# x's high halves made on ScalarE from raw x, and W's first chunk loaded by parts, in an FNet + GEGLU kernel

## The chip, the cores and the metric

One core of a Trainium2 chip runs the kernel. The metric is the device time of one execution in microseconds; the time before is the median of three runs. Names as in the profile: PE is TensorE's matmul, PEld its weight load, DVE VectorE, ACT ScalarE, POOL GpSimd, SP SyncE, whose queue issues the DMAs.

## The reference

```
h  = x + Real(DFT_seq(DFT_hidden(layernorm(x))))     x: 2048 x 448
     y = dft_seq_re @ a - dft_seq_im @ b,  a = ln @ dft_hid_re.T,  b = ln @ dft_hid_im.T
h2 = h + (gelu(ln(h) @ w_gate) * (ln(h) @ w_up)) @ w_down      w_gate, w_up: 448 x 1792
```

All in float32. The case here is the first product: the 2048 x 2048 sequence matrices (re and im), called W below, with the normalized x.

## The kernel before, in words

Float32 operands are split into two float16 halves, a high one (a rounded copy, made on ACT by `hi_part`, L103) and a low one (the difference, made on DVE by `lo_part`, L107 and L109). A product takes three matmuls: high by high, x's low by W's high, x's high by W's low (`TERMS`, L400).

The sequence transform runs in four batches of 512 output columns, each over 16 chunks of 128 rows of x (`N_STEPS` = 64 steps of the loop at L551). For each chunk the 448 columns of x are three blocks of 128 and a leftover of 64. `seq_mm` (L403) does the three blocks for both parts (re and im) in 18 matmuls of 128x512; `seq_mm_rest` (L418) does the leftover, in pairs that share PE. In the first batch x is loaded, normalized and split chunk by chunk, and kept in float16 for the other three batches; W is streamed in all four, two chunks of a batch sharing two 512 KB blocks (`seq_w`, L395: a chunk reads a part of both blocks). So chunk 6 needs the halves of blocks 6 and 7.

The order on every engine is written out by hand (`manual_schedule`). Ahead of the loop (L527 to L550) the first loads are issued (x tile 0, then the pieces of W's first two blocks and x tiles 1 and 2, then W's blocks 2 to 4) and the work of chunks 0 and 1 is interleaved. In the loop's step n, SP gets `x_load(n+3)` and `seq_load(n+5)`, and then, for the tiles ahead, come `x_norm(n+2)`, `seq_hi(n+3)`, `x_stats(n+3)`, `x_lo(n+2)`, `seq_lo(n+3)`. Steps 7, 9 and 11 also split the hidden transform's weights (`wh_split`, L455).

- `x_stats` (L340): mean and variance on DVE (L117, L118), the root on ACT (L124).
- `x_norm` (L344): on DVE the reciprocal and four small operations that refine it (`rstd`, L131 to L135) and the normalized x in place (`normed`, L140); on ACT x's high half from it.
- `x_lo` (L351): x's low half on DVE. x's raw tiles rotate through three buffers; the buffer of tile i is free after it.
- `first_load`, `first_hi`, `first_lo` (L374 to L393): blocks 0 and 1 of W in four pieces of 256 KB, by chunk and block, and their halves. These take two of the five buffers of W's raw blocks.

Chunks 0 to 2 are multiplied term by term over both parts (all high products first); from chunk 3 on part by part, with all three terms of a column block together, so the third matmul of such a chunk already reads W's low half. The leftover columns follow after chunks 1, 3, 7, 11 and 15.

Of the kernel before, what the change touches and what calls it, by code (L numbers as in the profile page):

```python
# [8 lines left out]
F16 = mybir.dt.float16  # L9
F32 = mybir.dt.float32  # L10
AF = mybir.ActivationFunctionType
ALU = mybir.AluOpType

P = 128
S, D, DF = 2048, 448, 1792
NT = S // P
# [6 lines left out]
EPS = 1e-5  # L23


X_SC = 16.0
D_SC = 64.0
# [5 lines left out]
def kernel(  # L33
# [35 lines left out]
    nc = tc.nc  # L69
    V, A, G, PE = nc.vector, nc.scalar, nc.gpsimd, nc.tensor  # L70
# [3 lines left out]
    small = ctx.enter_context(tc.tile_pool(name="small", bufs=3))  # L74
# [27 lines left out]
    def hi_part(dst, src, scale=1.0):  # L102
        A.activation(dst, src, AF.Copy, scale=scale)  # L103

    def lo_part(dst, src, hi, scale=1.0):
        if isinstance(scale, float) and scale == 1.0:
            V.tensor_sub(dst, src, hi)  # L107
        else:
            V.scalar_tensor_tensor(dst, src, scale, hi, op0=ALU.mult, op1=ALU.subtract)  # L109

    def stats(src, tag, pool=small):

        n = src.shape[1]
        mv = pool.tile([P, n, 2], F32, tag=f"mv{n}" if pool is small else f"mv_{tag}", name=f"mv_{tag}")
        for g in range(n):
            st = small.tile([P, 6], F32, tag="st", name=f"st_{tag}_{g}")
            V.bn_stats(st, src[:, g, :])  # L117
            V.bn_aggr(mv[:, g, :], st)  # L118
        return mv

    def root(mv, tag):
        n = mv.shape[1]
        sd = small.tile([P, n], F32, tag=f"sd{n}", name=f"sd_{tag}")
        A.activation(sd, mv[:, :, 1], AF.Sqrt, scale=1.0 / X_SC**2, bias=eps_t)  # L124
        return sd

    def rstd(mv, sd, tag, pool=small):

        n = sd.shape[1]
        r = pool.tile([P, 4, n], F32, tag=f"r{n}" if pool is small else f"r_{tag}", name=f"r_{tag}")  # L130
        V.reciprocal(r[:, 0], sd)  # L131
        V.tensor_scalar(r[:, 1], mv[:, :, 1], EPS, -0.5 / X_SC**2, op0=ALU.add, op1=ALU.mult)
        V.tensor_mul(r[:, 2], r[:, 0], r[:, 0])
        V.tensor_mul(r[:, 2], r[:, 2], r[:, 1])
        V.scalar_tensor_tensor(r[:, 3], r[:, 2], 1.5, r[:, 0], op0=ALU.add, op1=ALU.mult)  # L135
        return r[:, 3]

    def normed(dst, src, mv, r, g):

        V.tensor_scalar(dst, src, mv[:, g, 0:1], r[:, g : g + 1], op0=ALU.subtract, op1=ALU.mult)  # L140
# [147 lines left out]
    dft = right.enter_context(tc.tile_pool(name="dft", bufs=1, side="right"))  # L288
# [45 lines left out]
    xt, xs, norm_x = {}, {}, {}  # L334

    def x_load(i):
        xt[i] = dft.tile([P, 1, D], F32, tag="xt", bufs=3, name=f"x{i}")
        nc.sync.dma_start(xt[i][:, 0, :], x[i * P : (i + 1) * P, :])

    def x_stats(i):  # L340
        mv = stats(xt[i], f"x{i}")
        norm_x[i] = mv, root(mv, f"x{i}")

    def x_norm(i):  # L344
        mv, sd = norm_x.pop(i)
        xn = xt[i][:, 0, :]
        normed(xn, xn, mv, rstd(mv, sd, f"x{i}"), 0)
        xs[i] = dft.tile([P, 2, D], F16, name=f"xs{i}")
        hi_part(xs[i][:, 0], xn)

    def x_lo(i):  # L351
        lo_part(xs[i][:, 1], xt[i][:, 0, :], xs[i][:, 0])

# [1 line left out]
    wr, ws = {}, {}  # L357

    def seq_load(n):
        wr[n] = dft.tile([P, 8 * P], F32, tag="wr", bufs=5, name=f"wr{n}")  # L360
        b, q, jj = n // NT, n // 2 % 8, n % 2
        nc.sync.dma_start(wr[n], w_seq[(2 * b + jj) * 8 + q])

    def seq_hi(n):
        if n % 2 == 0:
            ws[n // 2] = dft.tile([P, 2, 2, 8 * P], F16, tag="ws", bufs=4, name=f"ws{n // 2}")
        hi_part(ws[n // 2][:, 0, n % 2], wr[n], D_SC)

    def seq_lo(n):
        t = ws[n // 2][:, :, n % 2]  # L370
        lo_part(t[:, 1], wr[n], t[:, 0], D_SC)


    def first_load(c, jj):  # L374
        if c == 0:
            wr[jj] = dft.tile([P, 8 * P], F32, tag="wr", bufs=5, name=f"wr{jj}")
        if c == jj == 0:
            ws[0] = dft.tile([P, 2, 2, 8 * P], F16, tag="ws", bufs=4, name="ws0")
        cols = slice(c * P, (c + 1) * P)
        nc.sync.dma_start(wr[jj].rearrange("p (b t) -> p b t", b=4)[:, :, cols], w_seq[jj * 8][:, :, cols])  # L380

    def first_views(c, jj):
        cols = slice(c * P, (c + 1) * P)
        ts = [wr[jj], ws[0][:, 0, jj], ws[0][:, 1, jj]]
        return [t.rearrange("p (b t) -> p b t", b=4)[:, :, cols] for t in ts]

    def first_hi(c, jj):
        src, hi, lo = first_views(c, jj)
        hi_part(hi, src, D_SC)

    def first_lo(c, jj):
        src, hi, lo = first_views(c, jj)
        lo_part(lo, src, hi, D_SC)  # L393

    def seq_w(n, l, part):  # L395

        t = ws[n // 2][:, l].rearrange("p a (r g c t) -> p r c a g t", r=2, g=2, c=2)
        return t[:, part, n % 2]

# [3 lines left out]
    def seq_mm(n, parts, terms=range(3)):  # L403

        b, c = divmod(n, NT)
        for part in parts:
            for k in range(3):
                for m in terms:
                    lx, lw = TERMS[m]
                    PE.matmul(  # L410
                        acc[b, 3 * part + k],
                        xs[c][:, lx, k * P : (k + 1) * P],
                        seq_w(n, lw, part),
                        start=c == 0 and m == 0,
                        stop=c == NT - 1 and m == 2,
                    )

    def seq_mm_rest(ns):  # L418

        for n in ns:  # L420
            b, c = divmod(n, NT)
            for m, (lx, lw) in enumerate(TERMS):
                for part in range(2):
                    PE.matmul(  # L424
                        acc[b, 6][64 * part : 64 * part + 64, :],
                        xs[c][:, lx, 3 * P :],
                        seq_w(n, lw, part),
                        start=c == 0 and m == 0,
                        stop=c == NT - 1 and m == 2,
                        skip_group_check=True,  # L430
                    )

    z = {}
# [67 lines left out]
    for k, f in enumerate(reversed(range(NF))):  # L501
        n = 17 + 3 * k
# [4 lines left out]
    for b in range(NB):  # L507
        for j in range(2):
            n = (b + 1) * NT + 1 + 6 * j
# [16 lines left out]

    x_load(0)  # L527
    for c in range(2):
        for jj in range(2):
            first_load(c, jj)  # L530
        x_load(c + 1)
    for n in range(2, 5):
        seq_load(n)
    x_stats(0)
    first_hi(0, 0)
    first_hi(0, 1)
    x_norm(0)
    first_lo(0, 0)
    x_lo(0)
    x_stats(1)  # L540
    first_lo(0, 1)
    first_hi(1, 0)
    first_hi(1, 1)
    x_norm(1)
    first_lo(1, 0)
    x_lo(1)
    first_lo(1, 1)
    seq_hi(2)
    x_stats(2)
    seq_hi(3)  # L550
    for n in range(N_STEPS):  # L551
        b, c = divmod(n, NT)
        if c == 0:
            for k in range(7):
                acc[b, k] = ps_seq.tile([P, TB], F32, tag="mm", name=f"acc{b}_{k}")
        if n + 3 < NT:
            x_load(n + 3)
        if n + 5 < N_STEPS:
            seq_load(n + 5)

        if n + 2 < NT:
            x_norm(n + 2)
        if 0 < n < N_STEPS - 3:
            seq_hi(n + 3)
        if n + 3 < NT:
            x_stats(n + 3)
        if n + 2 < NT:
            x_lo(n + 2)
        if n == 0:
            seq_lo(2)  # L570
        if n + 3 < N_STEPS:
            seq_lo(n + 3)
        for what in early.get(n, ()):
            what()
        if n < 3:
            for m in range(3):
                seq_mm(n, range(2), (m,))
        for part in range(2):
            if n >= 3:
                seq_mm(n, (part,))  # L580
            if c == NT - 1:
                for k in range(3 * part, 3 * part + 3):
                    z_out(b, k)
            for what in after.get((n, part), ()):
                what()

        if n in (1, 3) or n > 3 and c % 4 == 3:
            seq_mm_rest(range(n - 1 if n < 4 else n - 3, n + 1))
        if c == NT - 1:
            z_out(b, 6)  # L590
    gw = {f: gu[f].w for f in range(3)}
# [342 lines left out]
    for t in range(3 * NF, N_GU):  # L934
        f = t % NF
        if f < NF - 1:
            n, k = divmod(f, 2)
# [28 lines left out]
    for t in range(N_GU):  # L966
        q, f = divmod(t, NF)
# [58 lines left out]
    for i in range(4):  # L1026
        j, g = divmod(i, 2)
# [68 lines left out]
```

## Time and profile before

| | |
|---|---|
| median of three runs | 728.22 us (728.07 to 730.27) |
| the profiled execution | 729.39 us |
| its span | 727.6 us |
| first batch (16 chunks) | until about 81 us |
| ACT busy | 271.5 us (37%) |
| DVE busy | 500.1 us (69%) |
| TensorE's granted clock | 1.0 |

How to read it: a row of the timeline is the start in us from the start of the span, the duration, the engine, the line of the kernel, the operation, out<-in, shapes and the number of instructions merged; in brackets the idle time of the engine before it and what ended it. A row of the groups is line, engine, operation, out<-in, shapes and number, then busy us, mean ns of one, idle us before and what ended most of it. The chain of waits is followed back from the last instruction: start, duration, what. SPq is the queue that issues DMAs.

### The profile page before, as it was taken

Reading aid. Unit: us, or ns where it says so; the run is one execution under the profiler, and the core shown is the slowest. Engines: PE = TensorE matmul, PEld = TensorE weight load, DVE = VectorE, ACT = ScalarE, POOL = GpSimd, SP = SyncE. Lnnn points to the kernel's source line nnn. Section 1 sums busy time; section 2 is a strip of 40 time slices with the busy share of each in tenths; the row PEclk is TensorE's granted clock in tenths of the full one; section 3 lists DMA queues with packets and bytes.
Section 4 is the critical chain, followed back from the end, with each engine's and each line's share of the span. In section 5 each row is a group of like instructions: output and inputs, shape, how many; then the busy total and the mean of one; then the engine's idle time right before and its main releaser. Section 6 shows DMA issues by size and latency. Waiting matters only on the chain.

```text
span 727.6 us, 13421 instructions
## 1 busy us (share of the span) xinstructions
PE 719.5 (99%) x5330; PEld 499.2 (69%) x5330; DVE 500.1 (69%) x1026; ACT 271.5 (37%) x535; POOL 234.3 (32%) x274
## 2 busy tenths in 40 slices
PE   8999999999999999999999999999999999999998
PEld 5444444444444444444488889999999999999998
DVE  6888657486665866440477778788787877989730
ACT  4444704156133452221144443443444433454410
POOL 0000000000000001000057865577676766858430
PEclk9999999999999999999999999999999999999999
DMA  8766566577657976621057754757538496556411
GB/s 278 227 223 223 176 224 202 183 215 271 232 195 225 305 249 246 245 91 37 26 173 271 245 180 173 196 179 209 187 113 262 163 210 221 193 205 203 153 39 39
DMA packets 63518, 139.83 MB, mean 192 GB/s; under 512 B 30304, under 2 KB 39520, under 8 KB 63456
## 3 DMA queue, kind: packets, MB, share of 16 engines
q1 hardware_dynamic: 63456, 138.99, 58.0%
q8 instruction: 41, 0.67, 0.4%
q14 instruction: 21, 0.17, 0.1%
HBM read 112.23 MB, written 20.19 MB: 182 GB/s over the span
## 4 chain that ended last, share of the span: by engine, by line
PE 94%; DMA 3%; DVE 1%; ACT 1%; issue 0%; SPq 0%; DVEq 0%
PE acc L410 33%; PE pY L714 13%; PE acc_d L658 11%; PE y L475 9%; PE pX L714 9%; PE pZ L714 9%; PE acc L424 6%; DMA gw<-w_dram 2%; PE last_Y L877 1%; PE last_X L877 1%; PE last_tr L877 1%; DMA x<-in_x_dram 1%; PE last_a L877 1%; PE last_Z L877 1%; DMA wr<-in_w_seq_dram 1%; DVE ws L109 0%
## 5 line engine op out<-in xcount | busy, mean ns | idle before, releaser
L410 PE MATMUL acc<-ws,xs 128*128 128x512 f16 x1152 | 254.1, 379 | 0.9 <-ACT xs L103 0.6
L714 PEld LDWEIGHTS <-gw 128*128 128x128 f16 x2067 | 201.6, 98 | 24.9 <-DMA gw<-w_dram 2.1
L410 PEld LDWEIGHTS <-xs 128*128 128x128 f16 x1152 | 111.2, 98 | 139.6 <-issue 6.1
L714 PE MATMUL pY<-hops,gw 128*128 128x256 f16 x901 | 123.0, 273 | 1.6 <-DVE u L724 1.5
L658 PE MATMUL acc_d<-wd,dn_w 128*128 128x224 f16 x882 | 105.1, 259 | 0.0
L201 POOL TENSOR_TENSOR wd_s<-wd 128x448 f32<-128x448 f32 x7 | 7.9, 1131 | 274.1 <-DVE gu_w L109 274.1
L109 DVE SCALAR_TENSOR_TENSOR ws<-wr,ws 128x1024 f16<-128x1024 f32 (+1 forms) x66 | 77.9, 1187 | 15.2 <-ACT ws L103 15.2
L103 ACT ACTIVATE ws<-wr 128x1024 f16<-128x1024 f32 (+1 forms) x66 | 66.2, 1019 | 57.4 <-DMA wr<-in_w_seq_dram 28.0
L658 PEld LDWEIGHTS <-dn_w 128*128 128x128 f16 x882 | 85.1, 98 | 2.8
L714 PE MATMUL pX<-hops,gw 128*128 128x256 f16 x583 | 81.0, 273 | 1.0 <-DMA gw<-w_dram 0.9
L714 PE MATMUL pZ<-hops,gw 128*128 128x256 f16 x583 | 79.2, 273 | 0.0
L781 POOL TENSOR_TENSOR hh<-hh,g 128x256 f32<-128x256 f32 x42 | 31.0, 738 | 144.5 <-DVE hh L724 143.4
L724 DVE SCALAR_TENSOR_TENSOR u<-pY,u 128x256 f32<-128x256 f32 x112 | 46.9, 419 | 27.9 <-ACT c L788 19.0
L475 PE MATMUL y<-wh,z 128*128 128x448 f16 x336 | 65.7, 352 | 0.0
L483 DVE SCALAR_TENSOR_TENSOR hx<-y,hx 128x448 f32<-128x448 f32 x16 | 10.0, 625 | 78.1 <-PE y L475 78.1
L752 ACT ACTIVATE u<-pX 128x256 f32<-128x256 f32 x56 | 21.4, 383 | 90.9 <-PE pX L714 90.7
L475 PEld LDWEIGHTS <-z 128*128 128x128 f16 x336 | 32.8, 98 | 31.6 <-issue 0.4
L107 DVE TENSOR_TENSOR dn_w<-dn_s,dn_w 128x640 f16<-128x640 f32 x42 | 53.0, 1261 | 1.6 <-ACT dn_w L103 1.2
L765 ACT ACTIVATE g<-pX 128x256 f32<-128x256 f32 x56 | 21.4, 383 | 74.4 <-PE pX L714 69.1
L790 POOL TENSOR_TENSOR hh<-hh,c 128x256 f32<-128x256 f32 x42 | 40.8, 972 | 17.3 <-ACT c L788 17.1
L424 PE MATMUL acc<-ws,xs 128*64 128x512 f16 x384 | 44.7, 381 | 0.0
L807 POOL TENSOR_TENSOR dn_s<-hh 128x256 f32<-128x256 f32 x42 | 43.6, 1038 | 0.0
(107 smaller groups left out, 806.0 us busy)
## 6 DMA issues: line engine op xcount, KB each, us to landing
gw<-w_dram SPq DMA_DIRECT2D x53, 896.0 KB, 4.8
wr<-in_w_seq_dram SPq DMA_DIRECT2D x62, 512.0 KB, 5.9
w_dram<-gu_w SPq DMA_DIRECT2D x14, 896.0 KB, 4.7
gu_raw<-in_w_gu_dram SPq DMA_DIRECT2D x28, 384.0 KB, 5.8
wd<-in_w_down_dram SPq DMA_DIRECT2D x14, 448.0 KB, 5.4
x<-in_x_dram SPq DMA_DIRECT2D x16, 224.0 KB, 3.1
hx<-in_x_dram SPq DMA_DIRECT2D x8, 448.0 KB, 6.7
h_dram<-hx SPq DMA_DIRECT2D x8, 448.0 KB, 3.0
```

The costliest lines, as they stand in the source:

```text
L103: A.activation(dst, src, AF.Copy, scale=scale)
L107: V.tensor_sub(dst, src, hi)
L109: V.scalar_tensor_tensor(dst, src, scale, hi, op0=ALU.mult, op1=ALU.subtract)
L410: PE.matmul(acc[b, 3 * part + k], xs[c][:, lx, k * P : (k + 1) * P], seq_w(n, lw, part), start=c == 0 and m == 0, stop=c == NT - 1 and m == 2,
L424: PE.matmul(acc[b, 6][64 * part : 64 * part + 64, :], xs[c][:, lx, 3 * P :], seq_w(n, lw, part), start=c == 0 and m == 0, stop=c == NT - 1 ...
L475: PE.matmul(y[:, :D], z[b][:, lz, k, i * P : (i + 1) * P], wh[:, lw, k, :], start=k == 0 and m == 0, stop=k == 6 and m == 2,)
L658: PE.matmul(acc[k // 2][:, k % 2 * HD : (k % 2 + 1) * HD], a_of(la, a), b_of(lb, b), start=first and m == 0 and k % 2 == 0, stop=last and ...
L714: PE.matmul(ps, w[:, wl, wa + ws, :], ops[:, m + ms, :], start=first and n == 0, stop=last and n == len(terms) - 1, skip_group_check=True,)
L724: V.scalar_tensor_tensor(dst, ps, SC, other, op0=ALU.mult, op1=ALU.add)
L790: G.tensor_mul(c22, c22, self.c12)
L807: G.tensor_add(s[:, 0:2], t[:, 0:2], t[:, 2:4])
L877: PE.matmul(banks[0][:, c * HD : (c + 1) * HD] if one else banks[c][:, 0:HD], last["h"][:, lh, f, tok], w, start=f == 0 and m == 0 and c = ...
```

## The change

Three things change, all in the first batch.

W's blocks 0 and 1 are loaded in eight pieces of 128 KB, by chunk and part (re or im), into a tile of their own that takes the place of the later `z` tile; the five buffers of raw W blocks are left to blocks 2 and up. A part's halves are laid out next to each other.

x's high half is made by ACT straight from the raw tile, as Identity with a scale (1/deviation) and a bias (-mean/deviation) per partition, `x_hi`. The normalized x, which the low half is taken from, is made by a second such ACT operation in place, `x_norm`; for tile 0 it is made on DVE into a tile of its own. The small operations on DVE are four after the root in place of five, and one before it.

Chunks 0 to 5, and not 0 to 2, take all high products first; the leftover columns follow after chunks 0, 3, 7, 11 and 15.

```diff
     def x_stats(i):
         mv = stats(xt[i], f"x{i}")
-        norm_x[i] = mv, root(mv, f"x{i}")
+        sd = root(mv, f"x{i}")
+        r = small.tile([P, 5], F32, tag="rx", name=f"r_x{i}")
+        V.tensor_scalar(r[:, 1:2], mv[:, :, 1], EPS, -0.5 / X_SC**2, op0=ALU.add, op1=ALU.mult)
+        norm_x[i] = mv, sd, r
+    def x_rstd(i):
+        mv, sd, r = norm_x[i]
+        V.reciprocal(r[:, 0:1], sd)
+        V.scalar_tensor_tensor(r[:, 2:3], r[:, 0:1], r[:, 0:1], r[:, 1:2], op0=ALU.mult, op1=ALU.mult)
+        V.scalar_tensor_tensor(r[:, 3:4], r[:, 2:3], 1.5, r[:, 0:1], op0=ALU.add, op1=ALU.mult)
+        V.scalar_tensor_tensor(r[:, 4:5], mv[:, :, 0], -1.0, r[:, 3:4], op0=ALU.mult, op1=ALU.mult)
+    def x_hi(i):
+        r = norm_x[i][2]
+        xs[i] = dft.tile([P, 2, D], F16, name=f"xs{i}")
+        A.activation(xs[i][:, 0], xt[i][:, 0, :], AF.Identity, scale=r[:, 3:4], bias=r[:, 4:5])
     def x_norm(i):
-        mv, sd = norm_x.pop(i)
-        xn = xt[i][:, 0, :]
-        normed(xn, xn, mv, rstd(mv, sd, f"x{i}"), 0)
-        xs[i] = dft.tile([P, 2, D], F16, name=f"xs{i}")
-        hi_part(xs[i][:, 0], xn)
+        mv, sd, r = norm_x.pop(i)
+        x, xt[i] = xt[i][:, 0, :], xt[i][:, 0, :]
+        if i == 0:
+            xt[i] = dft.tile([P, 12 * P], F32, tag="raw", bufs=2, name="xn0")[:, :D]
+            normed(xt[i], x, mv, r[:, 3:4], 0)
+        else:
+            A.activation(xt[i], x, AF.Identity, scale=r[:, 3:4], bias=r[:, 4:5])
...
+    def first_load(c, part):
+        if c == part == 0:
+            wr["first"] = dft.tile([P, 2, 2, 4 * P], F32, tag="z", name="wr_first")
+            ws[0] = dft.tile([P, 2, 2, 8 * P], F16, tag="ws", bufs=4, name="ws0")
+        dst = wr["first"][:, part, c].rearrange("p (a g t) -> p a g t", a=2, g=2)
+        for jj in range(2):
+            nc.sync.dma_start(dst[:, jj], w_seq[8 * jj][:, 2 * part : 2 * part + 2, c * P : (c + 1) * P])
...
     x_load(0)
     for c in range(2):
-        for jj in range(2):
-            first_load(c, jj)
+        for part in range(2):
+            first_load(c, part)
         x_load(c + 1)
     for n in range(2, 5):
         seq_load(n)
     x_stats(0)
     first_hi(0, 0)
+    x_rstd(0)
+    x_hi(0)
+    x_norm(0)
     first_hi(0, 1)
-    x_norm(0)
-    first_lo(0, 0)
     x_lo(0)
     x_stats(1)
+    first_lo(0, 0)
+    first_hi(1, 0)
     first_lo(0, 1)
-    first_hi(1, 0)
+    x_rstd(1)
+    x_hi(1)
+    x_norm(1)
     first_hi(1, 1)
-    x_norm(1)
+    x_stats(2)
+    x_lo(1)
+    x_rstd(2)
+    x_hi(2)
+    x_norm(2)
     first_lo(1, 0)
-    x_lo(1)
     first_lo(1, 1)
     seq_hi(2)
-    x_stats(2)
     seq_hi(3)
...
-        if n + 2 < NT:
+        if 2 < n + 2 < NT:
+            x_rstd(n + 2)
+            x_hi(n + 2)
             x_norm(n + 2)
         if 0 < n < N_STEPS - 3:
             seq_hi(n + 3)
...
-        if n < 3:
+        if n < 6:
             for m in range(3):
                 seq_mm(n, range(2), (m,))
         for part in range(2):
-            if n >= 3:
+            if n >= 6:
                 seq_mm(n, (part,))
...
-        if n in (1, 3) or n > 3 and c % 4 == 3:
-            seq_mm_rest(range(n - 1 if n < 4 else n - 3, n + 1))
+        if n == 0 or c % 4 == 3:
+            seq_mm_rest(range(max(n - 3, min(n, 1)), n + 1))
```

More of the change, by code (lines that the diff above doesn't have):

```diff
@@ L341, in x_stats @@
         mv = stats(xt[i], f"x{i}")
-        norm_x[i] = mv, root(mv, f"x{i}")
-    def x_norm(i):
-        mv, sd = norm_x.pop(i)
-        xn = xt[i][:, 0, :]
-        normed(xn, xn, mv, rstd(mv, sd, f"x{i}"), 0)
-        xs[i] = dft.tile([P, 2, D], F16, name=f"xs{i}")
-        hi_part(xs[i][:, 0], xn)
+        sd = root(mv, f"x{i}")
[12 more added lines that the diff above has]
+        A.activation(xs[i][:, 0], xt[i][:, 0, :], AF.Identity, scale=r[:, 3:4], bias=r[:, 4:5])
+    def x_norm(i):
+        mv, sd, r = norm_x.pop(i)
[5 more added lines that the diff above has]
+            A.activation(xt[i], x, AF.Identity, scale=r[:, 3:4], bias=r[:, 4:5])
     def x_lo(i):
-        lo_part(xs[i][:, 1], xt[i][:, 0, :], xs[i][:, 0])
+        lo_part(xs[i][:, 1], xt[i], xs[i][:, 0])
     wr, ws = {}, {}
@@ L371, in seq_lo, with first_view, first_hi, first_lo @@
         lo_part(t[:, 1], wr[n], t[:, 0], D_SC)
[L374 to L377, printed above, removed]
+    def first_load(c, part):
+        if c == part == 0:
+            wr["first"] = dft.tile([P, 2, 2, 4 * P], F32, tag="z", name="wr_first")
             ws[0] = dft.tile([P, 2, 2, 8 * P], F16, tag="ws", bufs=4, name="ws0")
[L379 to L393, printed above, removed]
+        dst = wr["first"][:, part, c].rearrange("p (a g t) -> p a g t", a=2, g=2)
+        for jj in range(2):
+            nc.sync.dma_start(dst[:, jj], w_seq[8 * jj][:, 2 * part : 2 * part + 2, c * P : (c + 1) * P])
+    def first_view(l, c, part):
+        return ws[0].rearrange("p l a t -> p l (a t)")[:, l, (2 * part + c) * 4 * P :][:, : 4 * P]
+    def first_hi(c, part):
+        hi_part(first_view(0, c, part), wr["first"][:, part, c], D_SC)
+    def first_lo(c, part):
+        lo_part(first_view(1, c, part), wr["first"][:, part, c], first_view(0, c, part), D_SC)
     def seq_w(n, l, part):
+        if n < 2:
+            return first_view(l, n, part)
         t = ws[n // 2][:, l].rearrange("p a (r g c t) -> p r c a g t", r=2, g=2, c=2)
```

## The prediction

> **What bounds the kernel now.** I read the page first.
>
> ```profile
> span 727.6 us, 13421 instructions
> PE 719.5 (99%) x5330; PEld 499.2 (69%) x5330; DVE 500.1 (69%) x1026; ACT 271.5 (37%) x535; POOL 234.3 (32%) x274
> ```
>
> PE is busy for 719.5 of 727.6 us: 8.1 us of idle time is all that a better start can win, and a delay of PE is paid one for one. The change touches only the first of four batches (16 chunks, up to about 81 us), so I went to the chain of work that ended last.
>
> ```profile
> 7.54 7.23 DMA x<-in_x_dram
> ...
> 14.79 0.64 DVE st_x L117
> ...
> 20.94 3.84 PE acc L410 x17
> ...
> 34.54 7.50 PE acc L410 x34
> ```
>
> Two things are to be seen. Before 21 us the chain isn't PE's: it is the landing of x's fourth tile at 14.77, then DVE's queue in order (its statistics at 14.79, then the low part of tile 2, two low parts of W, and the reciprocal for tile 3 at 18.33, a row shown below). After that it is PE, but with one touch at 34.54: PE stood for the low part of W's chunk 7. So DVE is hardly ahead of PE. Why shows in the timeline of one step (chunk) of the loop:
>
> ```profile
> 18.33 0.15 DVE L131 RECIPROCAL r_x<-sd_x 128x1 f32<-128x1 f32 x1
> ...
> 22.35 0.16 DVE L131 RECIPROCAL r_x<-sd_x 128x1 f32<-128x1 f32 x1
> ...
> 22.93 0.16 DVE L135 SCALAR_TENSOR_TENSOR r_x<-r_x 128x1 f32<-128x1 f32 x1
> 23.12 0.51 DVE L140 TENSOR_SCALAR x<-x,mv_x,r_x 128x448 f32<-128x448 f32 x1
> 23.67 0.58 ACT L103 ACTIVATE xs<-x 128x448 f16<-128x448 f32 x1 [2.31 <-DVE x L140]
> 24.15 1.04 ACT L103 ACTIVATE ws<-wr 128x1024 f16<-128x1024 f32 x1
> 25.22 1.22 DVE L109 SCALAR_TENSOR_TENSOR ws<-wr,ws 128x1024 f16<-128x1024 f32 x1 [0.32 <-ACT ws L103]
> 26.36 0.15 DVE L131 RECIPROCAL r_x<-sd_x 128x1 f32<-128x1 f32 x1
> ```
>
> This is a ring between DVE and ACT: reciprocal, normalize, then on ACT x's high half (+1.32 after the reciprocal) and W's high half (+1.80), then on DVE W's low half (+2.87), and the next reciprocal behind it (+4.01). ACT waits 2.31 us of each step, but in this place it is part of the ring: what it gets longer there, the step gets longer.
>
> PE's own pace, from its timeline:
>
> ```profile
> 44.68 15.71 PE L410 MATMUL acc<-ws,xs 128*128 128x512 f16 x72
> 63.04 15.71 PE L410 MATMUL acc<-ws,xs 128*128 128x512 f16 x72
> ```
>
> Four chunks take 63.04 - 44.68 = 18.36 us, 4.59 per chunk, with 0.216 between two matmuls. A plain ring step is 4.0, but three steps also split the hidden weights:
>
> ```profile
> 42.44 0.16 DVE L131 RECIPROCAL r_x<-sd_x 128x1 f32<-128x1 f32 x1
> ...
> 48.19 0.16 DVE L131 RECIPROCAL r_x<-sd_x 128x1 f32<-128x1 f32 x1
> ...
> 66.59 0.16 DVE L131 RECIPROCAL r_x<-sd_x 128x1 f32<-128x1 f32 x1
> ```
>
> Step 7 takes 48.19 - 42.44 = 5.75, and step 9, with the same operations, is put at as much. From step 1 (18.33) to step 12 (66.59) are 48.26 us; less eight plain steps of 4.02 and these two, 4.6 are left for step 11 with the small last part. The ring's mean is 4.39, under PE's 4.59. An increase of 0.2 us per step makes the ring the bound of the batch.
>
> **The change, part by part.** The price of what moves to ACT stands in the groups by form, and one pair of such instructions in ACT's timeline:
>
> ```profile
> L103 ACT ACTIVATE xs<-x 128x448 f16<-128x448 f32 x16 | 9.2, 576 | 32.9 <-DVE x L140 32.8
> L222 ACT ACTIVATE xn_h<-hx,nb_h,r_h 128x448 f32<-128x448 f32 x8 | 5.7, 753 | 2.3 <-DVE nb_h L220 2.2
> L103 ACT ACTIVATE wh<-wh_raw,sign_t 128x448 f16<-128x448 f32 x1 | 0.7, 654 | 0.0
> 434.40 1.41 ACT L222 ACTIVATE xn_h<-hx,nb_h,r_h 128x448 f32<-128x448 f32 x2 [1.32 <-DVE nb_h L220]
> ```
>
> The same 128x448 costs 576 ns with constants, 654 with a scale per partition, 753 with scale and bias per partition. The new x_hi and x_norm are of the last kind (Identity, scale r[3], bias r[4]); x_hi writes f16, so its bounds are 0.58 and 0.75. I take 0.75, its nearest row by operands. Of two in a row the second starts 1.41 - 0.75 = 0.66 later. On the Trainium skill: its page "ScalarE: Activation LUTs", section "Step-by-step: what each stage is for", calls the scale and bias a free affine; taken at its word the two would cost the 576 of a copy. The rows speak against it, and so does the same page's section "What ACT_TABLE_LOAD costs", which adds about 93 ns for each per-partition operand; (753 - 576)/2 = 88 here.
>
> *The ring step after.* DVE: reciprocal, then three dependent small operations at the spacing of L135 and L140 above (0.19 each: 0.19, 0.39, 0.58), the last ends at +0.74. x_hi on ACT at +0.78, with the 0.04 from the end of L140 (23.63) to 23.67, until +1.53. x_norm overwrites the tile that x_hi reads, and in the changed program's order it waits for ACT itself: +1.56, not overlapped. W's high half 0.66 later, +2.22; W's low half 1.07 behind (24.15 to 25.22), +3.29, done at +4.52; the next reciprocal 1.14 behind its start, +4.43. So 4.42 for 4.01: the normalize that DVE saves (0.51) and a small product are more than eaten by 0.75 + 0.66 on ACT in place of 0.48. The low part of x (needs x_norm, +2.3) fits in front of W's low half. With the wh steps 0.41 longer each: 6.15, 6.15, 5.0.
>
> *The start.*
>
> ```profile
> 1.20 1.34 SPq L380 DMA_DIRECT2D wr<-in_w_seq_dram  x2
> 4.57 0.16 DVE L131 RECIPROCAL r_x<-sd_x 128x1 f32<-128x1 f32 x1 [0.36 <-ACT sd_x L124]
> 4.91 0.63 ACT L103 ACTIVATE ws<-wr 128x512 f16<-128x512 f32 x1 [0.38 <-DMA wr<-in_w_seq_dram]
> 5.17 1.48 SPq L362 DMA_DIRECT2D wr<-in_w_seq_dram  x3
> 5.76 0.63 ACT L103 ACTIVATE ws<-wr 128x512 f16<-128x512 f32 x1 [0.21 <-DMA wr<-in_w_seq_dram]
> 6.91 7.94 PE L410 MATMUL acc<-ws,xs 128*128 128x512 f16 x36 [0.61 <-ACT xs L103]
> 16.20 4.47 PE L410 MATMUL acc<-ws,xs 128*128 128x512 f16 x19
> 20.93 3.35 PEld L410 LDWEIGHTS <-xs 128*128 128x128 f16 x17 [0.56 <-DVE xs L107]
> GB/s 0 47 222 234 321 259 231 272 313 358 311 422 407 399 404 409 204 207 170 270 127 16 255 347 135 28 245 325 160 17 269 349 370 355 309 308 189 40 231 361
> DMA to landing us min/median/max: 3.7/5.4/8.1
> ```
>
> Now the first matmul needs both 256 KB pieces (the second's high half begins at 5.76). Afterwards it needs half of them, as many bytes as the first piece: high half at 4.91 to 5.54, x_hi at 5.45 (rstd done at 5.31) to 6.2, PE at 6.26, 0.65 earlier. The other part's high half is made until about 6.75 or 6.95, and PE wants it at 6.91. That gain doesn't last. ACT's queue now runs x_hi(1), x_norm(1), W(1,1), root(2), x_hi(2), x_norm(2) and only then the high halves of chunks 2 and 3, each 1.04: by the prices above they end near 16.3 (an estimate), and chunk 2's first matmul reads both, so PE starts chunk 2 about there, for 16.20 before. And the chain from x's fourth tile is untouched: SP issues it behind the same bytes. SP has four more pieces to issue at 0.67 (1.34 for two), so the three 512 KB loads begin at 5.17 + 2.7 = 7.9, the first lands no earlier than 3.7 (the shortest of such a load) later (11.6), and 1.25 MB more at 400 GB/s give 14.7 for x's fourth tile: 14.77 stands. Behind it one more small operation (0.13 to 0.2, the former L132 now sits before tile 2's low part): reciprocal of step 1 at 18.53 for 18.33. The term-major order for chunks 3 to 5 takes away PE's wait for tile 3's low part (0.56 at 20.93), yet chunk 3 can start only with x_hi(3) at 18.53 + 1.53 = 20.1, and now three chunks of leftover columns follow it in place of two: PE stands at chunk 4 about where it did. W's two early loads that no longer wait for a buffer (chunks 5 and 6) are read a whole step later or more and bring nothing. The matmuls are the same in number; leftover groups are two either way: 0.
>
> *Where the ring meets PE*, with reciprocals R from 18.53 on. Chunk 6 is part-major again, so its third matmul needs the low half of chunk 7, of step 4: 18.53 + 3 x 4.42 + 4.52 = 36.31, against 34.54: **+1.8**. Chunk 10's third needs step 8: R = 31.79 + 3 x 4.42 + 6.15 = 51.20, done 55.72; before it ran at 44.68 + 38 x 0.216 = 52.89: **+2.9**. Chunk 12 needs 51.20 + 4.42 + 6.15 + 4.52 = 66.29; PE comes at 63.04 + 0.43 + 2.9 = 66.4, no wait. Chunk 14's third needs step 12: 61.77 + 4.42 + 5.0 = 71.19, done 75.71, PE 75.75; before 63.04 + 38 x 0.216 = 71.25: **+4.5**. These are not added up, each contains the ones before it. Then x is used up, the ring ends with it, and ACT and DVE get ahead again. Nothing behind gives the delay back: PE is busy for 99% of the span.
>
> Sum: span 727.6 + 4.5 = 732.1. The profiled execution took 729.39, 1.2 over the median of the three runs, 728.22; on the median the forecast is **732.7**.
>
> **Rivals.**
> - *The pointers cost nothing*: x_hi and x_norm at 0.58, the step is 0.78 + 0.58 + 0.03 + 0.48 + 1.07 + 1.14 = 4.08. Chunk 7's low half is done at 18.53 + 12.24 + 4.17 = 34.94, PE 0.45 later than before, and no wait after it (chunk 11: 52.99, PE 53.3). 728.7. For it: x_hi writes f16. Against it: 753. Chance 0.06.
> - *Half of it*: 0.65 each, the row with one pointer: step 4.23, by the same meetings +1.05, +1.35, +2.2: 730.4. Chance 0.08.
> - *Not slower: the start's lead is kept.* The price is 0.65 at the first matmul, 0.56 at chunk 3 and, as an estimate, 0.2 at 34.54: 1.4 us, 726.8. It decides for this side if a step stays at or under 4.0 and x's fourth tile lands at or before 13.7; nothing in the rows shortens its queue. Chance 0.04. More than these 1.4 isn't there, so faster by over 0.3% (2.2 us, about what a measurement of this kernel can tell from no change) hardly can be.
> - *The pieces land late.* Eight pieces of half the size delay everything behind them: x's fourth tile 1 us later shifts the ring by 1 us: 733.7. The Trainium skill's page "DMA: Bandwidth & Descriptors", section "Measured (HBM→SBUF, 128 partitions, SWDGE, issued from GpSimd)", says to batch and shows less bandwidth for smaller transfers, which would point here; no run here shows 128 KB yet. Chance 0.07.
> - That the start gains nothing (PE still at 6.9) changes no number at the end, as the ring sets it.
>
> **How the numbers follow.** Forecast 732.7 with 0.75, its own range 731.7 to 734.2 (the step 0.08 shorter or longer, eleven times). The range takes in half pointers and late pieces: 730.2 to 734.6, leaving out free pointers, the kept lead and the tails. Chances: the forecast 0.73, the rivals as given, 0.02 for a gain from something not seen here. Slower is the forecast, late pieces and most of the half case: 0.86; same 0.12; faster 0.02.
>
> **What would show it.** The ring step in DVE's timeline, reciprocal to reciprocal: 4.42 (right), 4.0 to 4.1 (free). x_hi and x_norm at 0.75 in the groups, x_norm starting only when x_hi has ended. First matmul at 6.3. PE idle before chunk 6, 10 and 14 of about 1.9, 1.1 and 1.6 us, released by ACT's or DVE's ws. Wrong if tile 3 of x lands far from 14.8, if ACT lets x_norm overlap, or if PE's idle time stands somewhere behind 90 us.

## The result and the profile after

The change makes the kernel slower: 735.66 us (median of five runs, 735.47 to 736.77) against 728.48 (five runs, 728.07 to 730.27). The ratio is 1.0093, with a 95% interval of 1.0078 to 1.0108. The profiled execution of after took 736.77 with a span of 735.0; before's span was 727.6, so 7.4 us are to be found. The forecast had 4.5 of them.

The page of after, its span and busy times:

```profile
span 735.0 us, 13436 instructions
PE 721.2 (98%) x5330; PEld 499.8 (68%) x5330; DVE 497.2 (68%) x1011; ACT 285.2 (39%) x550; POOL 234.7 (32%) x274
```

PE has the same 5330 matmuls and is busy 1.7 us longer; its idle time went from 8.1 to 13.8. DVE did lose work (500.1 to 497.2), ACT got 13.7 more. Neither is near full, so it isn't the sums of work that decide. The groups of ACT by form, over the first 90 us:

```profile
L359 ACT ACTIVATE xs<-x,r_x 128x448 f16<-128x448 f32 x16 | 12.2, 761 | 28.6 <-DVE r_x L353 28.6
L369 ACT ACTIVATE x<-x,r_x 128x448 f32<-128x448 f32 x15 | 11.4, 762 | 0.5
```

Both new operations take 0.76, the f16 output no less than the f32 one. One step of the ring in the timeline of after, DVE and ACT in order of time:

```profile
24.20 0.15 DVE L350 RECIPROCAL r_x<-sd_x 128x1 f32<-128x1 f32 x1
24.39 0.22 DVE L351 SCALAR_TENSOR_TENSOR r_x<-r_x 128x1 f32<-128x1 f32 x1
24.64 0.16 DVE L352 SCALAR_TENSOR_TENSOR r_x<-r_x 128x1 f32<-128x1 f32 x1
24.84 0.16 DVE L353 SCALAR_TENSOR_TENSOR r_x<-mv_x,r_x 128x1 f32<-128x1 f32 x1
...
25.03 0.76 ACT L359 ACTIVATE xs<-x,r_x 128x448 f16<-128x448 f32 x1 [1.82 <-DVE r_x L353]
25.82 0.76 ACT L369 ACTIVATE x<-x,r_x 128x448 f32<-128x448 f32 x1
26.49 1.04 ACT L103 ACTIVATE ws<-wr 128x1024 f16<-128x1024 f32 x1
...
27.56 1.23 DVE L109 SCALAR_TENSOR_TENSOR ws<-wr,ws 128x1024 f16<-128x1024 f32 x1 [0.32 <-ACT ws L103]
28.71 0.16 DVE L350 RECIPROCAL r_x<-sd_x 128x1 f32<-128x1 f32 x1
```

Read the starts: 24.20, 25.03, 25.82, 26.49, 27.56, 28.71. A step takes 4.51 us (before 4.02). x_hi starts 0.83 after the reciprocal, x_norm 0.79 after x_hi, and from there on W's high and low halves follow as before. What the step costs PE stands in its timeline (a bracket: PE's idle time, and which tile's writer ended it):

```profile
36.61 0.59 PE L428 MATMUL acc<-ws,xs 128*128 128x512 f16 x2 [1.10 <-ACT ws L103]
37.87 7.50 PE L428 MATMUL acc<-ws,xs 128*128 128x512 f16 x34 [0.67 <-DVE ws L109]
...
56.40 0.59 PE L428 MATMUL acc<-ws,xs 128*128 128x512 f16 x2 [0.44 <-ACT ws L103]
57.66 7.50 PE L428 MATMUL acc<-ws,xs 128*128 128x512 f16 x34 [0.67 <-DVE ws L109]
...
76.78 0.59 PE L428 MATMUL acc<-ws,xs 128*128 128x512 f16 x2 [0.87 <-ACT ws L103]
78.04 7.50 PE L428 MATMUL acc<-ws,xs 128*128 128x512 f16 x34 [0.67 <-DVE ws L109]
...
88.19 2.12 PE L428 MATMUL acc<-ws,xs 128*128 128x512 f16 x9
```

PE stands before chunks 6, 10 and 14, as forecast, and the second batch begins at 88.19. (PE also stands 1.42 us before chunk 2, until 17.18, for ACT's high halves of W. It still waits for the ring at chunk 6, so this wait is covered there.) In before's timeline of PE it begins at 81.39:

```profile
78.68 2.78 PE L424 MATMUL acc<-ws,xs 128*64 128x512 f16 x24
81.39 2.98 PE L410 MATMUL acc<-ws,xs 128*128 128x512 f16 x13
```

So 6.8 of the 7.4 us have been lost by the end of the first batch. Where its ring began shows in after's chain of waits:

```profile
7.75 8.16 DMA x<-in_x_dram
15.93 0.64 DVE st_x L117
17.41 2.35 DVE ws L109 x2
19.77 0.08 DVE r_x L350
20.52 0.77 ACT xs L359
```

x's fourth tile lands at 7.75 + 8.16 = 15.91; in before it was 14.77. The ring starts 3.77 behind it, at 19.68. The queue that issues the loads (SPq, after):

```profile
1.21 1.95 SPq L400 DMA_DIRECT2D wr_first<-in_w_seq_dram  x4
3.21 0.47 SPq L338 DMA_DIRECT2D x<-in_x_dram  x1
3.72 1.97 SPq L400 DMA_DIRECT2D wr_first<-in_w_seq_dram  x4
5.73 0.47 SPq L338 DMA_DIRECT2D x<-in_x_dram  x1
6.24 1.38 SPq L382 DMA_DIRECT2D wr<-in_w_seq_dram  x3
7.75 0.50 SPq L338 DMA_DIRECT2D x<-in_x_dram  x1
```

Four small pieces are issued in 1.95 us, two pieces of twice the size took 1.34 in before. So the three 512 KB loads are issued from 6.24 and no longer from 5.17. x's fourth tile itself is issued only 0.21 later than before (7.54), but it lands 1.14 later, behind those loads.

The last 0.6 us arise later, where PE comes to the gate and up products. Before, then after, PE's timeline there:

```profile
381.57 0.83 PE L714 MATMUL pX<-hops,gw 128*128 128x256 f16 x6 [0.21 <-DMA gw<-w_dram]
```

```profile
389.31 0.83 PE L741 MATMUL pX<-hops,gw 128*128 128x256 f16 x6 [1.16 <-DMA gw<-w_dram]
```

PE waits there for a load of weights, 1.16 in place of 0.21; what follows gives a part back. This stretch differs from run to run: the same wait is 0.81 in e8_order_alone and 0.51 in e1_norm_on_dve, both below, and the second profiles of before and of after (e14, e12) have none and still part by 0.7 more between here and the end. From the start of the second batch to the end, two profiles of before differ by 0.5 us, and the runs below take between 1.4 us less and 1.6 us more than before, in no order that I can see. I didn't test what sets it, nor whether the edits have a part in it; these 0.6 us stay open.

### The profile page after: what moved, and what is told of

Read it like the earlier page. It is cut to its first block, busy times and chain, and to the rows that moved or that the text cites. A ratio compares the mean times of both kernels' runs of the same rounds, so it can differ in the third digit from the quotient of the medians.

```text
span 735.0 us, 13436 instructions
## 1 busy us (share of the span) xinstructions
PE 721.2 (98%) x5330; PEld 499.8 (68%) x5330; DVE 497.2 (68%) x1011; ACT 285.2 (39%) x550; POOL 234.7 (32%) x274
## 4 chain that ended last, share of the span: by engine, by line
PE 85%; DMA 5%; DVE 4%; ACT 3%; issue 1%; SPq 0%; DVEq 0%; ACTq 0%
PE acc L428 27%; PE pY L741 13%; PE acc_d L685 11%; PE y L493 9%; PE pZ L741 8%; PE pX L741 8%; PE acc L442 5%; DMA gw<-w_dram 2%; DVE ws L109 2%; ACT ws L103 1%; DMA x<-in_x_dram 1%; PE last_Y L904 1%; PE last_X L904 1%; PE last_tr L904 1%; ACT xs L359 1%
## 5 line engine op out<-in xcount | busy, mean ns | idle before, releaser
L109 DVE SCALAR_TENSOR_TENSOR ws<-wr,ws 128x1024 f16<-128x1024 f32 x62 | 75.3, 1221 | 16.1 <-ACT ws L103 16.1
L103 ACT ACTIVATE ws<-wr 128x1024 f16<-128x1024 f32 x62 | 63.7, 1046 | 56.9 <-DMA wr<-in_w_seq_dram 27.7
```

## The experiments

My theory after the result: two things add up. The ring of DVE and ACT starts 1.15 late, because four more issues on SP's queue delay the loads in front of x's fourth tile, and it runs at 4.51 per step. Rivals: that the late landing is due to the size of the transfers; that the loads cost nothing in the end and x on ACT is all of it; that the new order on PE costs something; that the in-place x_norm is the main part.

What the profile of each run shows, for the readings below. "Landing" is that of x's fourth tile, "start" the reciprocal for it, "step" a plain step of the ring, "batch 2" PE's first matmul of the second batch; the ratio is to runs of before on the same chip (medians 728.4 to 729.0).

| run | landing | start | step | batch 2 | time | ratio to before (95%) |
|---|---|---|---|---|---|---|
| before | 14.77 | 18.33 | 4.02 | 81.39 | 728.48 | 1 |
| after | 15.91 | 19.68 | 4.51 | 88.19 | 735.66 | 1.0093 (1.0078 to 1.0108) |
| e1_norm_on_dve | 15.30 | 19.08 | 3.75 | 81.86 | 730.07 | 1.0026 (1.0016 to 1.0036) |
| e2_x_as_before | 16.23 | 19.79 | 4.02 | 82.87 | 729.75 | 1.0023 (1.0013 to 1.0032) |
| e3_x_on_act_only | 14.29 | 19.49 | 4.51 | 87.93 | 736.54 | 1.0111 (1.0095 to 1.0127) |
| e4_norm_out_of_place | 15.59 | 19.36 | 4.37 | 86.12 | 734.3 | 1.0084 (1.0067 to 1.0101) |
| e5_loads_as_before | 14.01 | 18.88 | 4.51 | 87.35 | 734.47 | 1.0077 (1.0064 to 1.0091) |
| e6_x3_early | 11.86 | 18.46 | 4.51 | 86.92 | 733.54 | 1.0065 (1.0052 to 1.0077) |
| e8_order_alone | 14.08 | 17.80 | 4.02 | 80.88 | 729.18 | 1.0003 (0.9994 to 1.0012) |
| e10_best_try | 10.21 | 18.52 | 3.75 | 81.29 | 728.97 | 1.0003 (0.9994 to 1.0012) |
| e11_eight_pieces | 15.09 | 18.65 | 4.02 | 81.72 | 730.29 | 1.0018 (1.0005 to 1.0031) |
| e13_four_tiny_more | 15.87 | 19.44 | 4.02 | 82.50 | 730.32 | 1.0017 (1.0008 to 1.0027) |
| e12_after_again | 15.82 | 19.60 | 4.51 | 88.05 | 736.27 | one run |
| e14_before_again | 14.64 | 18.20 | 4.02 | 81.27 | 728.78 | one run |

**e1_norm_on_dve: x_norm taken off ACT.** After, with the normalized x made on DVE for every tile, into a tile of its own:

```diff
-        if i == 0:
-            xt[i] = dft.tile([P, 12 * P], F32, tag="raw", bufs=2, name="xn0")[:, :D]
-            normed(xt[i], x, mv, r[:, 3:4], 0)
-        else:
-            A.activation(xt[i], x, AF.Identity, scale=r[:, 3:4], bias=r[:, 4:5])
+        xt[i] = dft.tile([P, D], F32, tag="xn", bufs=2, name=f"xn{i}")
+        normed(xt[i], x, mv, r[:, 3:4], 0)
```

(W's raw blocks get four buffers in place of five, for the room.)

> The changed kernel with one part taken back: the normalized x is made on DVE again, from the raw tile into a tile of its own, for every tile, and x's high half stays on ACT. So one ACT operation of 0.76 us leaves the ring of DVE and ACT. (W's raw blocks get four buffers and not five, to make room.) Theory, the ring is the bound: the step falls from 4.51 to about 3.8 us, under PE's 4.59, PE never waits at chunks 6, 10 and 14, and what is left is the late landing of x's fourth tile (15.9 us): chunk 4 at about 27.5, 1.4 later than before, and 729.7 us, about 1.2 over before. Rival, the loads by parts cost most: nothing they do is changed here, so 734 or more. Rival, the order of the products in chunks 3 to 5 and of the leftover columns costs: also 734 or more.

The timeline of one of its steps:

```profile
30.33 0.16 DVE L350 RECIPROCAL r_x<-sd_x 128x1 f32<-128x1 f32 x1
...
31.05 0.51 DVE L140 TENSOR_SCALAR xn<-x,mv_x,r_x 128x448 f32<-128x448 f32 x1
...
31.16 0.76 ACT L359 ACTIVATE xs<-x,r_x 128x448 f16<-128x448 f32 x1 [1.86 <-DVE r_x L353]
31.83 1.04 ACT L103 ACTIVATE ws<-wr 128x1024 f16<-128x1024 f32 x1
...
32.95 1.22 DVE L109 SCALAR_TENSOR_TENSOR ws<-wr,ws 128x1024 f16<-128x1024 f32 x1
```

The 0.51 on DVE now runs beside x_hi, and W's high half follows x_hi directly (0.67). The step is 3.75, shorter than before's, PE doesn't stand at chunks 6, 10 and 14, and batch 2 begins 6.3 earlier than in after (0.6 of it because the ring starts earlier). So the second operation in ACT's part of the ring is the main cost; without it, x_hi from raw x makes the step shorter than before's.

**e4_norm_out_of_place: how much of it is the in-place wait.** After, x_norm on ACT as in the change but into a tile of its own:

```diff
+        xt[i] = dft.tile([P, D], F32, tag="xn", bufs=2, name=f"xn{i}")
         if i == 0:
-            xt[i] = dft.tile([P, 12 * P], F32, tag="raw", bufs=2, name="xn0")[:, :D]
             normed(xt[i], x, mv, r[:, 3:4], 0)
```

> The changed kernel with x_norm still on ACT but written to a tile of its own and not over the tile that x_hi reads (four buffers for W's raw blocks). Theory: what keeps x_norm 0.795 us behind the start of x_hi is that overwrite; it falls to 0.66, the ring step to 4.38, eleven steps give 1.4 us back: 734.2. If the 0.795 is ACT's own pace for such a pair, the step stays 4.51 and the time 735.7.

```profile
28.10 0.16 DVE L350 RECIPROCAL r_x<-sd_x 128x1 f32<-128x1 f32 x1
...
28.93 0.76 ACT L359 ACTIVATE xs<-x,r_x 128x448 f16<-128x448 f32 x1 [1.82 <-DVE r_x L353]
...
29.60 0.74 ACT L368 ACTIVATE xn<-x,r_x 128x448 f32<-128x448 f32 x1
30.25 1.04 ACT L103 ACTIVATE ws<-wr 128x1024 f16<-128x1024 f32 x1
...
32.47 0.15 DVE L350 RECIPROCAL r_x<-sd_x 128x1 f32<-128x1 f32 x1
```

x_norm starts 0.67 behind x_hi in place of 0.79, the step is 4.37 in place of 4.51. The in-place wait is thus 0.12 to 0.14 of the 0.49 by which the step grew: a part, not the main one.

**e3_x_on_act_only: x's part without the rest.** Before, with `x_stats`, `x_rstd`, `x_hi`, `x_norm` and `x_lo` as in after; loads and PE's order stay:

```diff
+    x_rstd(0)
+    x_hi(0)
     x_norm(0)
...
+    x_rstd(1)
+    x_hi(1)
     x_norm(1)
...
+            x_rstd(n + 2)
+            x_hi(n + 2)
             x_norm(n + 2)
```

> The kernel before with only x's high half and normalized x on ACT (x_rstd, x_hi, x_norm); loads and order of the products as before. Theory, the ring: x's fourth tile lands at 14.8, the ring starts at about 18.5 and takes 4.51 us per step, so chunk 14's third matmul comes at about 76.9 for 71.25 before: 5.6 us more, 734.1. Rivals, the loads or the order of the products: near before, 728.5 to 729.5.

The ring came as expected, the start didn't: x's fourth tile lands at 14.29, yet the reciprocal is at 19.49. DVE's timeline shows for what it waits:

```profile
16.68 0.62 DVE L107 TENSOR_TENSOR xs<-x,xs 128x448 f16<-128x448 f32 x1 [0.68 <-ACT x L369]
17.22 2.35 DVE L109 SCALAR_TENSOR_TENSOR ws<-wr,ws 128x1024 f16<-128x1024 f32 x2
19.49 0.15 DVE L350 RECIPROCAL r_x<-sd_x 128x1 f32<-128x1 f32 x1
```

DVE stands for ACT's x_norm of tile 2: ahead of the loop ACT's queue, with two operations of 0.76 per tile, has become the late one. So x's part alone costs as much as the whole change, and the parts don't add up: here ACT's queue holds back the ring's start, in after the landing does.

**e2_x_as_before: the rest without x's part.** After, with `x_stats`, `x_norm` and `x_lo` as in before, and `x_rstd` and `x_hi` empty:

```diff
     def x_norm(i):
-        mv, sd, r = norm_x.pop(i)
...
+        mv, sd = norm_x.pop(i)
+        xn = xt[i][:, 0, :]
+        normed(xn, xn, mv, rstd(mv, sd, f"x{i}"), 0)
+        xs[i] = dft.tile([P, 2, D], F16, name=f"xs{i}")
+        hi_part(xs[i][:, 0], xn)
```

> The changed kernel with x's statistics, normalization and high half as before (five small operations and the normalize on DVE, a copy of 0.58 us on ACT); the loads by parts and the order of the products stay. Theory, the ring: a step of 4.02 us again; the late fourth tile of x alone is left, PE about 1.1 us later at chunk 6, nothing at 10 and 14: about 729.6 us. Rivals, the loads or the order of the products: 734 or more, as in the changed kernel.

The ring is back at 4.02, the landing is late (16.23, the latest of all runs), batch 2 begins 1.5 late and the time is 0.23% longer. With the order of the products harmless (e8, below), that the loads cost nothing is thereby refuted: in this profile they cost about 1.5 us, with nothing else to cover them.

**e5_loads_as_before: the loads put back.** After, with W's first blocks in four pieces of 256 KB by chunk and block; the halves are still made by part:

```diff
-        dst = wr["first"][:, part, c].rearrange("p (a g t) -> p a g t", a=2, g=2)
-        for jj in range(2):
-            nc.sync.dma_start(dst[:, jj], w_seq[8 * jj][:, 2 * part : 2 * part + 2, c * P : (c + 1) * P])
+        dst = wr["first"][:, c, part].rearrange("p (b t) -> p b t", b=4)
+        nc.sync.dma_start(dst, w_seq[8 * part][:, :, c * P : (c + 1) * P])
```

> The changed kernel with W's blocks 0 and 1 loaded in four pieces of 256 KB again, by chunk and block as before (the halves are still made by part, read from two places); x on ACT and the order of the products stay. Theory: the four more issues on SP's queue are what makes the first 512 KB load be issued at 6.24 for 5.17 us and x's fourth tile land at 15.9 for 14.8; with four pieces it lands at about 14.8 again, the ring starts at 18.6 for 19.7, and all that follows comes 1.1 us earlier: 734.5. Rival, the later landing is chance or comes from something else of the change: 15.5 or later and 735.7.

Its issuing queue:

```profile
5.18 1.56 SPq L382 DMA_DIRECT2D wr<-in_w_seq_dram  x3
7.37 0.33 SPq L338 DMA_DIRECT2D x<-in_x_dram  x1
```

Time and step are as expected. With the 512 KB loads issued at 5.18 again, the landing is back (14.01), and the ring starts at 18.88, where I expected 18.6. The other 0.3 is DVE's own queue: it takes up the tile's statistics only at 15.14. Batch 2 comes 0.84 earlier than in after. That is what the pieces cost within this change; as times the two aren't told apart (the intervals overlap).

**e6_x3_early: the landing taken out of the way.** After, with x's fourth tile issued ahead of W's blocks 2 to 4 (four buffers for x, four for W's raw blocks):

```diff
+    x_load(3)
     for n in range(2, 5):
         seq_load(n)
...
-        if n + 3 < NT:
+        if 3 < n + 3 < NT:
```

> The changed kernel with x's fourth tile loaded ahead of W's blocks 2 to 4 and not behind them (four buffers for x's raw tiles, four for W's raw blocks). Theory: its landing at 15.9 sets the ring's start; it lands near 12 now, DVE is held by ACT's high halves of blocks 2 and 3 (done at about 17.1) and the ring starts at about 18.5 for 19.7: 734.5, with the step still 4.51. Rival, the start is set by ACT's queue alone: the ring starts at 19.7 and 735.7.

Now it lands at 11.86, four us early, and the ring starts at 18.46, only 1.2 earlier than in after. DVE's and ACT's timeline:

```profile
14.72 0.62 DVE L117 BATCH_NORM_STATS2 st_x<-x 128x6 f32<-128x448 f32 x1
...
15.09 1.99 ACT L103 ACTIVATE ws<-wr 128x1024 f16<-128x1024 f32 x2
...
16.19 2.36 DVE L109 SCALAR_TENSOR_TENSOR ws<-wr,ws 128x1024 f16<-128x1024 f32 x2
18.46 0.16 DVE L350 RECIPROCAL r_x<-sd_x 128x1 f32<-128x1 f32 x1
```

The statistics wait for nothing here and still come at 14.72; the queue of work ahead of the loop sets 18.5. So 18.53 was about the earliest this order allows. The time is 1 us below what I expected; batch 2 begins where it should (1.27 earlier than in after), and the rest arises behind the first batch, where the runs differ anyway.

**e11_eight_pieces and e13_four_tiny_more: size or number?** Before, each piece of 256 KB as two DMAs of 128 KB:

```diff
-        nc.sync.dma_start(wr[jj].rearrange("p (b t) -> p b t", b=4)[:, :, cols], w_seq[jj * 8][:, :, cols])
+        dst = wr[jj].rearrange("p (b t) -> p b t", b=4)
+        for h in (slice(0, 2), slice(2, 4)):
+            nc.sync.dma_start(dst[:, h, cols], w_seq[jj * 8][:, h, cols])
```

and before, with the four pieces as they are and behind each a DMA of 64 bytes into a tile that nothing reads:

```diff
+            spare = const.tile([1, 16], F32, name=f"spare{c}{jj}")
+            nc.sync.dma_start(spare, x[0:1, 0:16])
```

> The kernel before with only its four first pieces of 256 KB each loaded by two DMAs of 128 KB, in the same order; everything else as before. Theory, number of pieces: the first 512 KB load is issued about 1 us later, x's fourth tile lands at 15.3 to 16.2 as in the runs with eight pieces (14.0 to 14.8 with four), the ring starts as much later, and the time is 729.3 to 730. Rival, it is the order by part and not the number: x's fourth tile at 14.0 to 14.8 and 728.4.

> The kernel before with four more DMAs of 64 bytes among the first pieces (a piece of x's first row into tiles that nothing reads). It separates SP's time to issue from the transfers themselves. If the issues alone delay what stands behind them, the first 512 KB load is issued about 1.5 to 2 us later and x's fourth tile lands at 15.5 or later: 729.5. If it is the transfers in halves, x's fourth tile lands at 14.0 to 14.8: 728.4.

Both are slower by 0.17 to 0.18%; e11's landing, 15.09, is a little earlier than expected. The issuing queue of e13, in part:

```profile
4.56 0.47 SPq L532 DMA_DIRECT2D spare<-in_x_dram  x1
5.08 0.55 SPq L380 DMA_DIRECT2D wr<-in_w_seq_dram  x1
5.67 0.47 SPq L532 DMA_DIRECT2D spare<-in_x_dram  x1
...
6.58 1.37 SPq L362 DMA_DIRECT2D wr<-in_w_seq_dram  x3
```

A DMA of 64 bytes holds the queue for 0.47 us, about as long as one of 128 KB (1.95 for four). With four of them the 512 KB loads begin at 6.58, and x's fourth tile lands at 15.87, as in after. So four more issues are enough to delay it, with no transfer made smaller.

One landing isn't good to hundredths: the five profiles with before's four pieces and order of loads part by 0.76 (14.01 to 14.77), the six with eight pieces and that order by 1.14 (15.09 to 16.23). On their means the 512 KB loads are issued 1.06 later and x's fourth tile lands 1.30 later. Another rival is the load of W behind that tile, which after issues early (at 8.29, for 10.67 in before). It isn't that: e5 issues it at 7.74 and the tile lands at 14.01, e11 issues it at 10.76 and the tile lands at 15.09.

**e8_order_alone: PE's order.** Before, with chunks 0 to 5 term by term and the leftover after chunks 0, 3, 7, 11 and 15:

```diff
-        if n < 3:
+        if n < 6:
...
-        if n in (1, 3) or n > 3 and c % 4 == 3:
-            seq_mm_rest(range(n - 1 if n < 4 else n - 3, n + 1))
+        if n == 0 or c % 4 == 3:
+            seq_mm_rest(range(max(n - 3, min(n, 1)), n + 1))
```

> The kernel before with only the order of the products changed: chunks 0 to 5 all high products first, leftover columns after chunks 0, 3, 7, 11, 15. Theory, the ring: PE's wait at chunk 3 for x's low part (0.44) goes, chunk 6 still waits for W's block 7 until 34.5, so nothing is left of it: 728.2, within 0.3 us. Rival, this order costs: 729.5 or more.

PE's waits at chunks 3 and 6 are all but gone, batch 2 begins 0.5 earlier, and the time can't be told from before. The order does no harm. The 0.5 can't be put down to it: x's fourth tile happened to land 0.7 earlier here, and the ring started 0.5 earlier.

**e10_best_try: what is good of all.** e1's ring, the four pieces of e5 and e6's early load together.

> What the runs so far point to: the changed kernel with the normalized x on DVE into a tile of its own (ring step 3.75), W's first blocks in four pieces of 256 KB, and x's fourth tile loaded ahead of W's blocks 2 to 4. Theory: first matmul at about 6.9, the ring from about 18 on and faster than PE, no wait of PE at chunks 3, 6, 10 and 14: second batch at 80.5 for 81.4, 727.3. Rival, the start of the ring is held by something else: 728.5 to 730.

It missed: I expected a gain, and it is the same as before. The step is 3.75 and PE has no wait over 0.2 in the first batch, but batch 2 begins at 81.29, only 0.1 earlier than in before. The start of the ring is again held by DVE's queue ahead of the loop (18.52, with the tile landed at 10.21). That isn't all of it. From its first matmul to batch 2 PE takes 74.16 us here (7.13 to 81.29) and 74.48 in before (6.91 to 81.39), so the waits that went were worth only 0.3 us. Of the 0.8 that are missing against what I expected, 0.2 are the first matmul, which comes later. Another 0.5 PE still loses between 15.6 and 20.2, where three matmuls start 0.40, 0.32 and 0.43 behind the one before them, in place of 0.216; the last is the first of chunk 3, just behind the ring's start. No version here is faster than before.

**e12_after_again, e14_before_again.** The two kernels unchanged.

> The changed kernel once more, for a second landing of x's fourth tile: 15.3 to 16.2 if that is the piece's doing, and a ring step of 4.51.

> The kernel before once more, for a second landing of x's fourth tile: 14.0 to 14.8, and a ring step of 4.02.

The numbers repeat: landings 15.82 and 14.64, starts 19.60 and 18.20, steps 4.51 and 4.02, and 88.05 - 81.27 = 6.78 at batch 2.

## Why the prediction was right and wrong

The direction, the bound (the ring), the three places where PE meets it, and that nothing behind the first batch gives the delay back were right. The time was too low by 3 us, as two terms of the sum were too small at once: the delay of x's fourth tile, put at nothing, and the ring step. Point by point:

- **The price on ACT**: 0.75 forecast, 0.761 and 0.762 measured. Free pointers (576) and half of it (654) are refuted, for the f16 output too. The Trainium skill gives in "ScalarE: Activation LUTs", section "What ACT_TABLE_LOAD costs", 186 ns + 0.833 per element and 93 for each pointer operand: an estimate of 745 ns for two pointers and 448 elements, with which the trace agrees to 17 ns.
- **x_norm isn't overlapped with x_hi**: 0.78 forecast, 0.79 measured, 0.67 when it has a tile of its own (e4).
- **The ring step**: 4.42 forecast, 4.51 measured, so 0.09 short, a little more than the 0.08 that the forecast's own range allowed. 0.05 of it lies in the small operations: the first product (L351) took 0.22 and not 0.16, and x_hi starts 0.83 and not 0.78 after the reciprocal. The rest is hundredths in each link of the ring. From step 1 to step 12 it adds up: 73.39 - 19.68 = 53.71 for the forecast's 52.66, which is **1.05**.
- **"14.77 stands"**: this is the step that failed. I saw that the 512 KB loads would be issued later, and let the first of them land 3.7 us after its issue, the shortest figure in the row of DMAs. It took 6.5, as it had in before (5.17 to 11.63), and between 5.6 and 6.9 in the fourteen profiles. So the later issue was passed on: landing at 15.91, ring start at 19.68 for 18.53, **1.15**. The row that should have been used was that very load's own time, not the minimum over all loads. A second error went the other way: I priced the four more issues at 0.67 each, the price of 256 KB, and had the loads begin at 7.9; they began at 6.24. The two partly cancelled, which was luck: with 7.9, that load's own 6.5 and my 3.1 for the bytes behind it, the tile would have landed at 17.5. The forecast's own sign of being wrong, a landing far from 14.8, came true.
- **The sum**: 4.5 + 1.15 + 1.05 + 0.09 (W's low half of a step done 4.65 after its reciprocal for 4.56 at chunk 14) = 6.79, and batch 2 is late by 88.19 - 81.39 = 6.80. The remaining 0.6 of the span arises behind the first batch, where runs differ.
- **The rival of late pieces** (733.7, chance 0.07) described the failed step with its size, 1 us. The reason it gave, less bandwidth for smaller transfers, isn't needed: e13 has the delay with pieces of 256 KB. I had put it beside the forecast as another way to go, and the range took in either; but nothing excludes that a late landing and a longer step come together, and they did. 732.7 + 1.15 + 1.05 is already 734.9, past the range's end of 734.6.
- **The first matmul**: 6.3 forecast, 6.81 measured and 7.25 in e12. x_hi was done at 6.42; PE was still at work on its transposes at the start (L97), which end at 6.3 in one profile of before and at 7.4 in the other (e14). As said, it changes nothing at the end.
- **Chunk 2**: ACT's high halves were put near 16.3 and chunk 2 with them; they were done at 17.13 and PE began it at 17.18. DVE had stood 1.41 us for x's third tile, until 11.36. The later wait at chunk 6 covers this too.
- **PE's idle time** before chunks 6, 10 and 14: 1.9, 1.1 and 1.6 forecast; by the brackets 1.10 + 0.67, 0.44 + 0.67 and 0.87 + 0.67, so 1.77, 1.11 and 1.54, released by ACT's and DVE's ws: right. The meetings themselves came at 37.87, 57.66 and 78.04, or 3.3, 4.8 and 6.8 behind before (34.54, 52.89, 71.25) for the 1.8, 2.9 and 4.5 forecast: 1.5, 1.9 and 2.3 more, which is the late start and about 0.1 for each step since.
- **"Not slower"** is refuted: the step would have had to stay at 4.0 and the landing at 13.7; both went the other way.

## What to carry to other kernels

Two engines that are 39% and 68% busy can still set the time when they wait for each other in a ring: price a moved operation by the link of the ring that it lengthens, not by the engine's busy time (x_hi alone on ACT made the step 0.27 shorter, x_norm behind it 0.76 longer). Split a load only after counting what each further issue does to the loads behind it on the same queue. And when two dangers can come true together, add them in the range.

## What the runs showed of the hardware

- At the start of the kernel a DMA of 64 bytes held SP's queue for 0.46 to 0.49 us (e13), one of 128 KB for 0.42 to 0.47 (after), one of 256 KB for 0.55 to 0.68 and one of 512 KB for 0.43 to 0.53 (before): the time doesn't follow the size. The Trainium skill's "DMA: Bandwidth & Descriptors", section "Anatomy of one DMA — SWDGE (gpsimd) path", has about 50 ns for the sequencer's dispatch, which is one part of an issue and on another path than this queue; no run here splits an issue into parts.
- The first 512 KB load took 5.6 to 6.9 us from issue to landing in fourteen profiles, whether issued at 5.17 or at 6.71, with loads queued in front of it each time. Why it is so nearly constant stays open.
- The ring starts 3.56 (x's stage as before) or 3.77 us (as in after) behind the landing of x's fourth tile wherever that lands at 14.6 or later. Where it lands earlier, the start doesn't follow: it stays between 17.8 and 19.5, set by the queues of DVE and ACT ahead of the loop.
- A scalar_tensor_tensor of 128x1 took 0.22 us where its scalar is a column of the tile (L351), 0.16 where it is a constant (L352).
